# Experts 1 to 7 and the overflow tile in scaled f16 pairs, with the order of three engines in the experts laid down

## The chip, the cores and the metric

The kernel runs on one core of one Trainium2 chip. The metric is the device time of one execution in microseconds (us). TensorE multiplies (PE in the profile), ScalarE is ACT, VectorE is DVE, GpSimd is POOL, and SyncE (SP) issues most transfers.

## What is computed

Three blocks run one after the other: attention with a decay for 4 x 8 heads of 576 tokens, a swiglu layer for 2304 tokens, and a mixture of 8 experts in which each token goes to one expert. In the reference, cut to the last block:

```python
# x: 2304 x 512, w1: 8 x 512 x 1024, w2: 8 x 1024 x 512, all float32
logits = x @ w_gate
expert_idx = np.argmax(logits, axis=1)
probs = softmax(logits)
for e in range(8):
    mask = expert_idx == e
    h = np.maximum(x[mask] @ w1[e], 0.0)
    out[mask] = gate_w[mask, None] * (h @ w2[e])
```

`gate_w` is the probability of the chosen expert. The swiglu's output is `x` here, and everything is float32 in and out.

## The kernel before

**Up to 703 us** the kernel does the attention and the swiglu in 9 groups of 256 tokens; the order of its instructions is set by a list scheduler with its own estimates of times. As each group's swiglu is done, `fin0` copies its rows (ys, L711 and L712) and stores them as f32 in y_d; `fin1` and `fin2` turn them (yt), multiply by the gate's weights, take the best expert and give each token a place in a list of slots. From 703 to 727 us the last group is routed while TensorE works on the first 128 tokens of expert 0 (`filler`, L1152 to L1183).

**The experts** run in a loop over s = 0 to 8. An expert has 320 places, as tiles of 128, 128 and 64 rows; what does not fit goes to the overflow tile, s = 8. All products are made from pairs: a float32 value is split into a high part rounded to fp32r and a rest, and three products (high by high, high by low, low by high) are added. `mm1` makes the hidden layer h: for each of 8 blocks fk of 128 hidden values, 12 matmuls of 320 columns (L1347; 192 for expert 0), then ScalarE writes relu (L1352) and VectorE the rest in two pieces (L1354). `mm2` multiplies h by w2 for the three row tiles in 24, 24 and 16 matmuls of 512 columns (L1390); ScalarE scales the result by the gate into o (L1392, L1394), GpSimd scatters it to the output (L1136). There is one h buffer; three banks of PSUM turn for mm1, three for mm2.

**The weights** come as f32 in four pieces of 512 KB per matrix (two matrices an expert) into four buffers (wr, issued by SP); ScalarE copies the high part (L1101), VectorE subtracts the rest (L1102). **The tokens** of the next expert are gathered from y_d by GpSimd (L1204), their 16-bit words separated by GpSimd and VectorE (L1468), turned by DMA (L1471), put together by ScalarE and VectorE (L1475, L1476) and split (L93). For experts 0 and 1 TensorE turns them (L1215). For the overflow tile `gate_of` (L1483) works out the gate again.

The scheduler orders the loop too: it mixes the L1347 of one expert with the L1390 of the one before, and places the relus, copies and splits where its estimates put them.

## Time and profile before

| | us |
|---|---|
| median of 3 executions | 986.05 (984.83 to 986.61) |
| the profiled execution | 986.64 |
| its span in the trace | 984.8 |
| TensorE busy in the span | 901.6 (92%) |
| VectorE busy | 624.5 (63%) |
| ScalarE busy | 551.1 (56%) |
| attention and swiglu, up to the last group's routing | 703 |
| last routing, beside the filler | 703 to 727 |
| expert 0 and the entry to expert 1 | 727 to 757 |
| the rest of the experts and the overflow tile | 757 to 974 |
| last copy, scatter and end | 974 to 985 |

Times in rows are microseconds from the span's start. Matmuls are pipelined: the duration printed for one is longer than the distance to the next one, so a stream is priced by its length in the chain of waits over its count. An engine that is busy for almost all of a stretch sets its length; the others matter there only where something waits for them.

### The profile page before, as it was taken

What the parts mean: (1) busy time and instruction counts of PE and PEld (TensorE: products, weight loads), DVE (VectorE), ACT (ScalarE), POOL (GpSimd) and SP (SyncE); (2) the same over time, 40 slices, a digit from 0 to 9 for tenths busy, and PEclk for the clock granted to TensorE, in tenths of its full rate; (3) what the DMA queues carried; (4) which work ended last, traced back from release to release, by engine and by line L of the source; (5) the groups of instructions that cost most, each with busy time, mean ns of one, the idle gap of its engine ahead of it and who ended that gap; (6) DMA issues with size and microseconds to landing.
All of it is one profiled execution on the core that took longest, in us unless ns stands there. A gap on an engine that the chain in (4) does not pass through costs nothing.

```text
span 984.8 us, 20192 instructions
## 1 busy us (share of the span) xinstructions
PE 901.6 (92%) x7317; PEld 751.1 (76%) x7317; DVE 624.5 (63%) x1876; ACT 551.1 (56%) x1210; POOL 302.6 (31%) x366
## 2 busy tenths in 40 slices
PE   3688669879999999999999999999999999999995
PEld 2466447667788888888878788888888878988884
DVE  7998999888657555666643535445547676556540
ACT  6999997667566656666633322223425554555440
POOL 0110125336434434344442232232256432110011
PEclk9999777989999999999999999999999999999998
DMA  8615868889787687577655502102369875665410
GB/s 238 186 39 153 208 165 180 158 167 190 144 159 142 113 165 150 104 142 127 102 106 135 150 23 56 32 8 80 99 169 246 231 219 159 184 209 193 141 57 35
DMA packets 265496, 136.92 MB, mean 139 GB/s; under 512 B 228943, under 2 KB 241359, under 8 KB 265394
## 3 DMA queue, kind: packets, MB, share of 16 engines
q1 hardware_dynamic: 261136, 125.23, 54.6%
q0 software_dynamic: 4064, 10.24, 3.5%
q8 instruction: 58, 0.95, 0.4%
q14 instruction: 44, 0.36, 0.1%
q10 hardware_dynamic: 194, 0.14, 0.1%
HBM read 84.76 MB, written 10.82 MB: 97 GB/s over the span
## 4 chain that ended last, share of the span: by engine, by line
PE 42%; DMA 9%; issue 7%; DVE 3%; ACT 1%; POOL 1%; SPq 0%; POOLq 0%; DVEq 0%; ACTq 0%
PE yp L663 10%; PE v L601 9%; PE g L601 9%; PE bank L1347 4%; PE bank L1390 3%; DMA pair<-words 3%; DMA out_dram<-o,ix 3%; PE ps L322 1%; DMA pt<-p 1%; PE px L485 1%; DMA xg<-y_d,ix 1%; DVE wlo L1102 1%; DMA xr<-xs 1%; DVE wolo L1102 1%; PE ps L327 1%
## 5 line engine op out<-in xcount | busy, mean ns | idle before, releaser
L422 POOL TENSOR_TENSOR p<-st,p 128x128 f16<-128x128 f32 (+1 forms) x96 | 82.0, 857 | 115.2 <-issue 65.2
L648 POOL TENSOR_TENSOR lo<-t,hi 128x512 fp32r<-128x512 f32 x54 | 70.8, 1312 | 134.3 <-ACT hi L647 102.7
L601 PE MATMUL g<-xr,wga 128*128 128x256 f16 x864 | 104.6, 278 | 1.1 <-DVE t L634 1.1
L601 PE MATMUL v<-xr,wva 128*128 128x256 f16 x864 | 103.1, 273 | 0.6 <-DVE p L454 0.6
L389 ACT ACTIVATE st<-st,nb,c 128x64 f32<-128x64 f32 (+4 forms) x160 | 102.8, 645 | 1.4
L379 DVE CUSTOM_DVE_ANT_0 st<-ps,zero 128x64 f32<-128x64 f32 (+3 forms) x160 | 55.8, 376 | 70.5 <-PE ps L332 64.8
L601 PEld LDWEIGHTS <-wga 128*128 128x128 f16 x864 | 83.7, 100 | 17.6 <-issue 6.4
L601 PEld LDWEIGHTS <-wva 128*128 128x128 f16 x864 | 83.8, 100 | 10.2 <-issue 0.6
L631 ACT ACTIVATE t<-g,gscale 128x512 f32<-128x512 f32 (+3 forms) x72 | 39.4, 572 | 79.6 <-PE g L601 77.8
L419 DVE CAST p<-st 128x448 f16<-128x448 f32 (+3 forms) x120 | 48.7, 412 | 34.6 <-ACT st L389 32.8
L433 POOL TENSOR_TENSOR p<-st,p 128x64 f16<-128x64 f32 x96 | 43.0, 448 | 79.4 <-issue 34.9
L1136 POOL DMA_INDIRECT out_dram<-o,ix x24 | 24.8, 1033 | 126.5 <-ACT o L1392 81.6
L647 ACT ACTIVATE hi<-t 128x512 fp32r<-128x512 f32 x54 | 33.7, 624 | 52.0 <-DVE t L641 51.9
L322 PE MATMUL ps<-qkt 128*128 128x64 f16 (+4 forms) x288 | 53.7, 288 | 7.8 <-DVE mx L379 4.7
L663 PE MATMUL yp<-wohi,hi 128*128 128x512 f32 x144 | 59.5, 413 | 0.0
L1352 ACT ACTIVATE h<-bank 128x320 fp32r<-128x320 f32 (+1 forms) x64 | 26.1, 422 | 57.8 <-PE bank L1347 57.5
L1354 DVE SCALAR_TENSOR_TENSOR h<-bank,h 128x64 fp32r<-128x64 f32 (+2 forms) x128 | 33.4, 305 | 39.1 <-ACT h L1352 39.0
L663 PE MATMUL yp<-wohi,lo 128*128 128x512 f32 x144 | 56.9, 395 | 0.0
L663 PE MATMUL yp<-wolo,hi 128*128 128x512 f32 x144 | 56.3, 391 | 0.0
L327 PE MATMUL ps<-cum,nc 128*128 128x64 bf16 (+2 forms) x192 | 55.2, 294 | 0.0
L385 ACT ACTIVATE nb<-mx,addc,c 128x3 f32<-128x3 f32 (+1 forms) x64 | 24.7, 386 | 52.4 <-DVE mx L379 51.9
L641 DVE SCALAR_TENSOR_TENSOR t<-t,hscale,v 128x512 f32<-128x512 f32 (+3 forms) x72 | 42.4, 609 | 16.1 <-PE v L601 15.7
(372 smaller groups left out, 2554.5 us busy)
## 6 DMA issues: line engine op xcount, KB each, us to landing
wr<-in_moe_w_dram SPq DMA_DIRECT2D x72, 512.0 KB, 5.0
vr<-in_v_dram SPq DMA_DIRECT2D x16, 288.0 KB, 3.9
qk_in<-in_q_dram SPq DMA_DIRECT2D x32, 128.0 KB, 2.9
qk_in<-in_k_dram SPq DMA_DIRECT2D x32, 128.0 KB, 2.8
v_in<-in_v_dram SPq DMA_DIRECT2D x32, 128.0 KB, 2.7
y_d<-ys SPq DMA_DIRECT2D x6, 512.0 KB, 4.1
wgb<-in_moe_w_gate_dram SPq DMA_DIRECT2D x5, 512.0 KB, 5.2
raw<-in_moe_w_val_dram SPq DMA_DIRECT2D x5, 512.0 KB, 5.1
```

Of the source, the lines that this page charges most:

```text
L322: pe.matmul(out=ps[:, o:o + n], lhsT=lq[:, 128 * j:128 * j + 128], rhs=rk_[:, k0:k1], start=(x == 0), stop=False, skip_group_check=True,)
L327: pe.matmul(out=ps[:, o:o + n], lhsT=pk, rhs=cum3[:, k0 - 64:k1 - 64], start=False, stop=(k1 <= d0), skip_group_check=True,)
L379: vec.tensor_tensor_reduce(out=sts[m][:, k0 - 64:k1 - 64], in0=ps[:, o:o + n], in1=zero.to_broadcast([128, n]), scale=1.0, scalar=init, op ...
L389: act.activation(out=sts[m], in_=sts[m], func=ACTF.Exp, scale=c[:, 0:1], bias=nb[:, m:m + 1], accum_out=sm[:, m, hh:hh + 1],)
L419: vec.tensor_copy(out=flat[:, o + 64:o + 64 + n], in_=src)
L422: gp.tensor_tensor(out=flat[:, o1:o1 + n - 64], in0=src[:, 64:n], in1=flat[:, o + 128:o + 64 + n], op=ALU.subtract)
L433: gp.tensor_tensor(out=blk[:, :, 0:64], in0=pair, in1=blk[:, :, 64:128], op=ALU.subtract)
L601: pe.matmul(out=ps[:, fi, :], lhsT=w16[:, kk, wi, 128 * fi:128 * fi + 128], rhs=xr[:, kk, x0:x0 + 2, xi, :], start=(n_ == 0), stop=(n_ == ...
L631: act.activation(out=t[:, :, c0:c1], in_=gps[:, :, c0:c1], func=ACTF.Tanh, scale=gscale[:, b, j:j + 1])
L641: vec.scalar_tensor_tensor(out=t[:, :, c0:c1], in0=t[:, :, c0:c1], scalar=hscale[:, b, j:j + 1], in1=vps[:, :, c0:c1], op0=ALU.mult, op1=A ...
L648: last["lo"] = gp.tensor_tensor(out=lo, in0=t, in1=hi.bitcast(F32), op=ALU.subtract)
L663: pe.matmul(out=yps[g][i], lhsT=hx[:, fi, 128 * i:128 * i + 128], rhs=wo[fk][wx], start=(j in opens and n_ == 0), stop=(j in shuts and n_ ...
```

## The change

**Number format.** For experts 1 to 7 and the overflow tile the pairs become f16. To stay in the range of f16 each matrix is multiplied by a power of two. `load16` holds the steps: `square` sums the squares of a quarter of the matrix (ScalarE L1148, or VectorE L1143), `reduce` adds the four sums (VectorE L1155), `total` adds over partitions with a matmul of one column (TensorE L1159), `scale` takes the exponent with three small VectorE operations, and `convert` writes the high half (ScalarE L1170, a copy with a scale) and the low half (VectorE L1171). Expert 0 stays in fp32r.

**Tokens.** `fin1` sums the squares of each token's row (ScalarE, two operations a group), and `halves` writes both f16 halves of the row (two operations on ScalarE L748, two on VectorE L749) and stores them to a new array y16_d, 2304 x 1024 f16, 4.7 MB in all. Experts 1 and on gather from y16_d, and one DMA transpose per tile puts both halves in place: the separation of words, xf, the split and the TensorE transposes for expert 1 are gone. `gates` multiplies the gate by the inverse scales. The overflow's gate takes 4 matmuls and 4 transposes in place of 16 matmuls.

**Order.** In the expert stage `laid` ties every instruction of TensorE, ScalarE and VectorE to the one before it in the program's order. `plan` says after which block of mm1 (list a) and after which eight matmuls of mm2 (list b) squares, totals and conversions stand. SP and GpSimd are not tied.

**Buffers.** Raw weights stay in three places of one matrix each: the four wr buffers and two that held expert 0's w1 (free after expert 0's mm1). There are two token buffers, three o buffers and four f16 matrix pairs.

The diff, cut to its core:

```diff
+    y16_d = dram.tile([NT + 1, 2 * DM], F16, name="y16_d")
...
+    def halves(g, ys, yt, sc):
+        yh = yt.rearrange("p i k t -> p (i k t)").bitcast(F16).rearrange("p (i c) -> p i c", i=2)
+        for i in range(2):
+            hi = yh[:, i, 0:DM]
+            act.activation(out=hi, in_=ys[:, i, :], func=ACTF.Copy, scale=sc[:, i:i + 1])
+            vec.scalar_tensor_tensor(
+                out=yh[:, i, DM:], in0=ys[:, i, :], scalar=sc[:, i:i + 1], in1=hi, op0=ALU.mult, op1=ALU.subtract
+            )
+        rows_out(y16_d, g, yh)
...
+        sq = M["rt"].tile([128, 2, 2], F32, tag="ysq", name="ysq")
+        for i in range(2):
+            jk = M["rt"].tile([128, G], F32, tag="lgp", name="jk", bufs=1).bitcast(F16)
+            act.activation(out=jk, in_=ys[:, i, :], func=ACTF.Square, accum_out=sq[:, 0, i:i + 1])
+        exponent(sq[:, 1, :], sq[:, 0, :], sq[:, 0, :], 20, 11)
+        ytp[g] = (yt, lg, ys, sq)
...
+        if g < NG - 1:
+            halves(g, ys, yt, sq[:, 1, :])
...
+        if g == NG - 1:
+            halves(g, ys, yt, sq[:, 1, :])
...
+        act.dma_start(out=y16_d[NT:NT + 1, :], in_=zr.bitcast(F16))
...
+    def load16(s, which, src, psum, e_i=None):
+        n, cols = src.shape[-2] // 128, src.shape[-1]
+        step, k16 = 1024 // cols, len(turns16)
+        turns16.append((s, which))
+        q4 = EP["wq"].tile([128, 4], F32, tag="q4", name="q4")
+        sc = EP["wq"].tile([128, 1], F32, tag="wsc", name="wsc")
+        inv = inv16[s, which] = EP["winv"][:, k16 % 4:k16 % 4 + 1]
+        raw, stage = [], stages[(k16 - 2) % 3] if k16 > 1 and (k16 - 2) % 3 < 2 else None
...
+        def square(i, on_vec=False):
+            t = raw[i][1].rearrange("p k c -> p (k c)")
+            acc = q4[:, i:i + 1]
+            if on_vec:
+                jk = jd[0]
+                vec.tensor_tensor_reduce(
+                    out=jk, in0=t, in1=t, scale=1.0, scalar=0.0, op0=ALU.mult, op1=ALU.add, accum_out=acc
+                )
+            else:
+                jk = EP["wq"].tile([128, 1024], F16, tag="ja", bufs=1, name="ja")
+                act.activation(out=jk, in_=t, func=ACTF.Square, accum_out=acc)
+
+        tot = []
+
+        def reduce():
+            tot.append(EP["wq"].tile([128, 1], BF16, tag="qs", bufs=2, name="qs"))
+            with nc.allow_low_precision(reason="only picks a power of two"):
+                vec.tensor_reduce(out=tot[0], in_=q4, axis=AX.X, op=ALU.add)
+
+        def total():
+            tot.append(psum()[:, 0:1])
+            pe.matmul(out=tot[1], lhsT=ones, rhs=tot[0], start=True, stop=True, skip_group_check=True)
+
+        def scale():
+            exponent(sc, inv, tot[1], 20, 7 if which == 1 else 1)
+
+        def convert(i):
+            c, t = raw[i]
+            wt[s, which] = [
+                bufs16[k16 % 4][:, x].rearrange("p (k c) -> p k c", k=n) for x in range(2)
+            ]
+            h_, l_ = [x[:, c:c + step, :] for x in wt[s, which]]
+            act.activation(out=h_, in_=t, func=ACTF.Copy, scale=sc)
+            vec.scalar_tensor_tensor(out=l_, in0=t, scalar=sc, in1=h_, op0=ALU.mult, op1=ALU.subtract)
...
-                    EP["w1"] = [go() for go in load_w(1, 1, w1[1])]
+                    EP["w1"] = load16(1, 1, w1[1], lambda: ps_s.tile([128, 512], F32, tag="s", name="tot"))
+                    for i in range(4):
+                        EP["w1"]["sq"](i)
+                    for x in ("red", "mm", "exp"):
+                        EP["w1"][x]()
             elif g1 == NG - 1 and j1 == NJ - 1:
-                wbuf.append([wpa.tile([128, 4096], F32R, tag=x, name=x) for x in ("wga", "wva")])
+                bufs16.extend(wpa.tile([128, 2, 4096], F16, tag=x, name=x) for x in ("wga", "wva"))
                 with tc.issue_after(last["hi"].ins):
-                    for f_ in EP["w1"]:
-                        f_()
-                EP["w12"] = [go() for go in load_w(1, 2, w2[1])]
+                    for i in range(4):
+                        EP["w1"]["cv"](i)
...
+            if beat and n_ % 8 == 7 and n_ < len(prods) - 1:
+                beat()
...
-    def turn(xt, xs):
-        pair = tw_p.tile([128, 2 * KD, CAP], U16, tag="pair", name="pair")
+        return gather(xg_p, idx, None, y16_d if s else y_d)
+
+    def turn(s, xs):
         o = 0
-        for t, (x, n, _) in enumerate(xs):
-            words = tw_p.tile([128, 2, DM], U16, tag="words", name="words", bufs=2)
-            for w in range(2):
-                (gp, vec)[w].tensor_copy(
-                    out=words[0:n, w, :], in_=x[0:n, :].bitcast(U16).rearrange("p (d w) -> p d w", w=2)[:, :, w]
-                )
-            sp.dma_start_transpose(out=pair[:, :, o:o + n], in_=words[0:n].rearrange("p w d -> p (w d)"))
+        for x, n, _ in xs:
+            sp.dma_start_transpose(out=x16[s % 2][:, :, o:o + n], in_=x[0:n, :])
             o += n
-        xf = hs_p.tile([128, KD, CAP], F32, tag="hs", name="xf")
-        xw = xf.bitcast(U16).rearrange("p k (t w) -> p k t w", w=2)
-        act.activation(out=xw[:, :, 0:o, 0], in_=pair[:, 0:KD, 0:o], func=ACTF.Copy)
-        vec.tensor_copy(out=xw[:, :, 0:o, 1], in_=pair[:, KD:, 0:o])
-        split(xt[0][:, :, 0:o], xt[1][:, :, 0:o], xf[:, :, 0:o], xt[0][:, :, 0:o].bitcast(F32))
...
+    def plan(s):
+        m1, m2, m3 = 2 * s, 2 * s + 1, 2 * s + 2
+        a, b = [[[] for _ in range(9)] for _ in range(2)]
+        if s == 0:
+            a[1] = [("sq", 1, 0), ("sq", 1, 1, True)]
+            a[2] = [("sq", 1, 2), ("sq", 1, 3, True)]
+            a[4] = [("red", 1)]
+            a[6] = [("mm", 1)]
+            a[7] = [("exp", 1)]
+            b[0] = [("cv", 1, 0), ("cv", 1, 1)]
+            b[1] = [("cv", 1, 2), ("cv", 1, 3)]
+            b[3] = [("sq", 2, 0), ("sq", 2, 1, True)]
+            b[4] = [("sq", 2, 2), ("sq", 2, 3, True)]
+        else:
+            for i in range(4):
+                a[2 * i] = [("cv", m1, i)]
+                a[2 * i + 1] = [("sq", m2, i)]
+                b[3 + i] = [("cv", m2, i)]
+            if s == 1:
+                a = [
+                    [("red", 2), ("sq", 3, 0)], [("sq", 3, 1)], [("mm", 2), ("sq", 3, 2)], [("exp", 2), ("cv", 2, 0)],
+                    [("cv", 2, 1)], [("cv", 2, 2)], [("cv", 2, 3)], [("sq", 3, 3)],
+                ]
+            b[0] = [("sq", m3, 0), ("sq", m3, 1, True)]
+            b[1] = [("red", m2), ("sq", m3, 2), ("sq", m3, 3, True)]
+            b[2] = [("mm", m2)]
+            b[3].insert(0, ("exp", m2))
+            b[4] += [("red", m3)]
+            b[6] += [("mm", m3)]
+            b[7] += [("exp", m3)]
+        return a, b
...
+                    tc.add_manual_dep(
+                        ins, before[ins.engine].name,
+                        mybir.DependencyInfo(mybir.DependencyClass.NoSync, mybir.DependencyReason.DATA), reason="laid",
+                    )
+                before[ins.engine] = ins
...
+                mm1(fk, wt[s, 1], xt, bank, h, 0 if s else 128)
+                do(*pa.pop(0))
+                if fk == 3 and nxt is not None:
+                    turn(nxt, xgs[nxt])
+            if s:
+                ask(2 * s + 3)
...
+            stages.extend(EP["wq0"].tile([128, 4096], F32, tag=f"w{x}0", name="stage") for x in ("hi", "lo"))
+            ask(2)
+            ask(3)
...
```

ScalarE between one expert and the next, before (bank is PSUM; L1352 is the relu, L1394 the copy of the 64-row tile, L1101 and L1475 weights and tokens of later experts):

```order
L1352 ACTIVATE h<-bank_10515 128x320
L1394 ACTIVATE o<-bank_10503 64x512
L1352 ACTIVATE h<-bank_10495 128x320
L1352 ACTIVATE h<-bank_10511 128x320
...
L1101 ACTIVATE whi_9035<-wr 128x1024 x4
L1352 ACTIVATE h<-bank_10515 128x320
L93 ACTIVATE xh_10472<-xf 128x1280
L1475 ACTIVATE xf<-pair 128x1280
L1101 ACTIVATE wohi<-wr 128x1024 x2
L1392 ACTIVATE o<-bank_10507,ixf 128x512
```

and after (L1457 is the relu, L1170 a conversion, L1148 a square, L1505 and L1507 the copies to o):

```order
L1507 ACTIVATE o<-bank_10658 64x512
L1457 ACTIVATE h<-bank_10666 128x320
L1170 ACTIVATE wohi<-stage,wsc 128x1024
L1457 ACTIVATE h<-bank_10670 128x320
L1148 ACTIVATE ja,q_11372<-wr 128x1024
L1457 ACTIVATE h<-bank_10650 128x320
...
L1148 ACTIVATE ja,q_11518<-stage 128x1024 x2
L1505 ACTIVATE o<-bank_10662,sx_10636 128x512
L1170 ACTIVATE wolo<-wr,wsc 128x1024 x2
```

Relus stood in a row with the weights' copies in bunches; now one piece of weight work stands between any two relus, and each relu waits behind it.

TensorE where mm2 of one expert meets mm1 of the next, before:

```order
L1347 MATMUL bank_10515<-xh_10472,wva 128x320
L1390 MATMUL bank_10507<-whi_9035,h 128x512
L1390 MATMUL bank_10507<-wlo_9036,h 128x512
L1390 MATMUL bank_10499<-whi_9035,h 128x512
L1390 MATMUL bank_10499<-wlo_9036,h 128x512
...
L1347 MATMUL bank_10495<-xh_10472,wga 128x320
L1347 MATMUL bank_10495<-xl_10473,wga 128x320
```

and after (L1501 is mm2, L1159 the total, L1452 mm1; weight loads have rows of their own in f16):

```order
L1501 MATMUL bank_10658<-wva,h 128x512
L1159 LDWEIGHTS ones
L1159 MATMUL bank_10678<-qs,ones 128x1
L1501 LDWEIGHTS h
...
L1452 LDWEIGHTS wohi
L1452 MATMUL bank_10670<-x_0_10633,wohi 128x320
...
L1452 MATMUL bank_10650<-x_0_10633,wohi 128x320
```

Before, matmuls of two experts and of several row tiles were mixed; now mm1 runs block by block to its end, then mm2 tile by tile, with a total in between.

VectorE in the last group's routing, before (L712 and L754 are copies that the routing needs, L1102 weight work, L784 the first step of taking the best expert):

```order
L1102 TENSOR_TENSOR wva<-wr,wga 128x1024 x3
L712 COPY ys<-yp 128x512
L1102 TENSOR_TENSOR wva<-wr,wga 128x1024
L754 COPY yt<-ps 128x512
L784 TENSOR_REDUCE rmx<-ps 128x2
L786 SCALAR_TENSOR_TENSOR oh_10336<-ps,rmx,desc 128x8 x2
```

and after (the same steps are L713, L1171, L778, L815 and L817; L732 to L740 are the exponent, L749 the low halves):

```order
L1171 SCALAR_TENSOR_TENSOR wga<-wr,wsc,wga 128x1024
L713 COPY ys<-yp 128x512
L1171 SCALAR_TENSOR_TENSOR wga<-wr,wsc,wga 128x1024 x3
L778 COPY yt<-ps 128x512
L732 TENSOR_SCALAR ysq<-ysq 128x2
L737 TENSOR_SCALAR ysq<-ysq 128x2
L740 TENSOR_SCALAR ysq<-ysq 128x2
L749 SCALAR_TENSOR_TENSOR yt<-ys,ysq,yt 128x512
L815 TENSOR_REDUCE rmx<-ps 128x2
L749 SCALAR_TENSOR_TENSOR yt<-ys,ysq,yt 128x512
L817 SCALAR_TENSOR_TENSOR oh_10484<-ps,rmx,desc 128x8 x2
```

Three pieces of weight work instead of one stand between the copies ys and yt, and the halves stand on both sides of the step that takes the best expert.

## Rows read from the trace of the kernel before

**Rows 1.** Windows: stretch, length; busy (count) PE, PEld, DVE, ACT, POOL; clock, DMA share, GB/s.
```profile
0.00:160.00 160.00, 108.08 (x944) 78.05 (x945) 147.24 (x466) 143.16 (x368) 21.86 (x33) 0.87 0.63 165
220.00:545.00 325.00, 319.44 (x3137) 266.13 (x3136) 193.74 (x597) 192.27 (x479) 137.00 (x188) 1.00 0.71 138
545.00:703.00 158.00, 157.74 (x1268) 132.25 (x1268) 72.47 (x356) 42.54 (x77) 42.24 (x39) 1.00 0.22 58
703.00:727.00 24.00, 23.13 (x128) 17.63 (x125) 13.16 (x47) 10.58 (x17) 8.73 (x10) 1.00 0.51 139
727.00:757.00 30.00, 28.99 (x185) 26.56 (x186) 18.36 (x37) 15.09 (x24) 20.40 (x20) 0.94 0.81 204
757.00:974.00 217.00, 212.54 (x1156) 188.44 (x1156) 125.97 (x228) 104.32 (x147) 44.89 (x46) 1.00 0.57 170
```

**Rows 2.** Chain of waits, matmul streams at full clock: start, us, what, count.
```profile
347.77 2.64 PE g L601 x24
...
792.72 5.28 PE bank L1347 x36
...
890.23 11.71 PE bank L1390 x50
...
936.29 1.68 PE bank L1483 x16
```

**Rows 3.** TensorE timeline of an f16/bf16 stream: start, us, line, op, tiles, shapes, count.
```profile
221.08 0.60 PE L322 MATMUL ps<-qkt 128*128 128x512 f16 x2
221.52 0.38 PE L327 MATMUL ps<-cum,nc 128*128 128x512 bf16 x1
221.73 0.19 PE L332 MATMUL ps<-maskgt,negid 128*128 128x64 bf16 x1
```

**Rows 4.** TensorE's waits in 757 to 974: waiter, releaser: us in total, times, longest.
```profile
PE bank L1390 <- ACT h L1352: 2.7, 3, 1.5
PE bank L1390 <- DVE h L1354: 2.1, 4, 1.1
```

**Rows 5.** Groups by shape, 757 to 974: count | busy us, mean ns | idle before.
```profile
L1352 ACT ACTIVATE h<-bank 128x320 fp32r<-128x320 f32 x55 | 23.2, 436 | 47.5 <-PE bank L1347 47.2
...
L1101 ACT ACTIVATE wga<-wr 128x1024 fp32r<-128x1024 f32 x20 | 19.9, 1051 | 2.4 <-PE bank L1390 1.4 <-PE bank L1347 1.0
```

**Rows 6.** f16 weight work of the swiglu, by line: count, min/median/max ns.
```profile
L1016 ACT ACTIVATE wga<-c x4: 614/619/639, 19.1 to 108.3; 128x512 f16<-128x512 f32 x4
...
L1016 ACT ACTIVATION_READ_ACCUMULATOR wga<-c x4: 185/192/210, 19.6 to 108.8; 128x1 f32 x4
...
L1030 ACT ACTIVATE wga<-c,sw x4: 706/707/708, 35.9 to 126.2; 128x512 f16<-128x512 f32 x4
...
L1031 DVE SCALAR_TENSOR_TENSOR wga<-c,sw,wga x4: 733/738/743, 39.7 to 129.2; 128x512 f16<-128x512 f32 x4
```

**Rows 7.** VectorE timeline, last routing.
```profile
706.56 3.82 DVE L1102 TENSOR_TENSOR wva<-wr,wga 128x1024 fp32r<-128x1024 f32 x3 [1.65 <-ACT wga L1101]
...
710.31 0.68 DVE L712 COPY ys<-yp 128x512 f32<-128x512 f32 x1
...
712.04 0.68 DVE L754 COPY yt<-ps 128x512 f32<-128x512 f32 x1
```

**Rows 8.** ScalarE timeline, last routing.
```profile
709.28 0.57 ACT L711 ACTIVATE ys<-yp 128x512 f32<-128x512 f32 x1
```

**Rows 9.** TensorE timeline, entry to the experts.
```profile
727.08 0.58 PE L1347 MATMUL bank<-xh,whi 128*128 128x192 f32 x3 [0.47 <-ACT xh L93]
...
733.56 0.99 PE L1215 MATMUL bank<-ident,xg 128*128 128x128 f32 x8
```

**Rows 10.** DMA issues of the page: KB each, median us to landing.
```profile
wr<-in_moe_w_dram SPq DMA_DIRECT2D x72, 512.0 KB, 5.0
```

**Rows 11.** ScalarE timeline, first 20 us.
```profile
9.59 0.63 ACTq L919 DMA_DIRECT2D y_d<-zr  x1
...
14.14 0.66 ACT L998 ACTIVATE c<-raw 128x512 f32<-128x512 f32 x1 [1.03 <-DMA raw<-in_moe_w_gate_dram]
```

More of the change, by code (lines that the diff above doesn't have):

```diff
@@ L845, in fin2 @@
         if final:
-            place(0, 1)
+            place(0, NT3)
         step(g)
         if final:
-            vec.tensor_tensor(out=EP["ix"], in0=ixf[:, 0, :], in1=rk[:, 32:32 + NT3], op=ALU.add)
+            vec.tensor_tensor(out=EP["ix"], in0=ixf[:, 0:NT3], in1=rk[:, 32:32 + NT3], op=ALU.add)
         vec.tensor_tensor(out=cnt, in0=cnt, in1=rk[:, 2 * NE:3 * NE], op=ALU.add)
@@ L1340, with f32 @@
     LO = CAP + 64
+    def f32(x):
+        return x.bitcast(F32) if x.dtype == F32R else x
     def mm1(fk, w, x, ps, h, c0):
@@ L1375, in mm1s, with mm2 @@
             hi = hh[:, f0:f0 + 4, 0:128]
-            split(hi, hl[:, f0:f0 + 4, 0:128], p, hi.bitcast(F32))
-    def mm2(t, n, idx, gwt, w, hh, hl, ps, o_p):
+            split(hi, hl[:, f0:f0 + 4, 0:128], p, f32(hi))
+    def mm2(t, n, idx, gwt, w, hh, hl, ps, o_p, beat=None):
         p = ps("m2")
@@ L1417, in table @@
             )
-            tc.keep_in_program_order(first)
             oe = ov.tile([1, NE], F32, name="oe")
@@ L1452, in weights @@
         src = w1 if which == 1 else w2
-        return load_w(s, which, src[s]) if s < NE else load_w(s, which, src, reg["e"])
+        if s < NE:
+            return load16(s, which, src[s], lambda: banks[7])
+        return load16(s, which, src, lambda: banks[7], reg["e"])
     def fetch_x(s, t0=0):
@@ L1483, in gate_of @@
             pe.matmul(
-                out=p, lhsT=x[:, kk, 0:128].bitcast(F32), rhs=rg[:, kk, 0:NE], start=(n_ == 0),
+                out=p, lhsT=f32(x[:, kk, 0:128]), rhs=rg[:, kk, 0:NE], start=(n_ == 0),
                 stop=(n_ == len(prods) - 1), skip_group_check=True,
@@ L1495, in gate, with ask, do @@
     def gate(s, t):
-        return ixf[0:ROWS[t], 1, TPE * s + t:TPE * s + t + 1] if s < NE else gwo
+        n = ROWS[t] if s < NE else 128
+        return sx[s % 2][0:n, t:t + 1] if s else ixf[0:n, 2 * NE * TPE + t:2 * NE * TPE + t + 1]
+    asked = {}
+    def ask(m):
+        if m < 2 * NE:
+            asked[m] = weights(m // 2 + 1, m % 2 + 1)
+    def do(*items):
+        for what, m, *i in items:
+            if m in asked:
+                asked[m][what](*i)
+    def plan(s):
[11 more added lines that the diff above has]
+            b[4] = [("sq", 2, 2), ("sq", 2, 3, True)]
+        else:
+            for i in range(4):
[15 more added lines that the diff above has]
+        return a, b
@@ new lines, in laid @@
+    def laid():
+        body = nc.cur_bb.bb.instructions
+        before = {}
+        for ins in list(body)[n_before:]:
+            if ins.engine in LAID and not type(ins).__name__.startswith("BassTile"):
+                if ins.engine in before:
+                    tc.add_manual_dep(
+                        ins, before[ins.engine].name,
+                        mybir.DependencyInfo(mybir.DependencyClass.NoSync, mybir.DependencyReason.DATA), reason="laid",
+                    )
+                before[ins.engine] = ins
@@ L1510 @@
             sp.dma_start(out=ixo, in_=id_d[bass.ds(reg["r"], 128), :])
[L1511 to L1549 removed]
+    laid()
     p2.close()
```

204 lines of the change are left out of this document (131 added, 73 removed).

## The prediction, made before the change was run

> **What bounds the kernel now.** I read the windows first [rows 1]. From 220 us on TensorE is busy 97 to 100% of every stretch, at a granted clock of 1.00 except just after the entry to the experts (0.94). In the experts (757 to 974) it works 212.54 of 217 us; VectorE works 126, ScalarE 104, the DMA engines 57%. So the length of the expert stage is the number of matmuls times the distance between two of them, and the other engines count only where TensorE waits for them. Up to 160 us it is otherwise: ScalarE and VectorE work 143 and 147 of 160 us. Second, the waits: in those 217 us TensorE waits 4.8 us in all, for a relu or its rest [rows 4]. Third, the chain of waits gives lengths of unbroken streams, and so the distance [rows 2]: mm1 5.28/36 = 146.7 ns for 320 columns of fp32r, mm2 11.71/50 = 234.2 ns for 512 columns, and the swiglu's f16 2.64/24 = 110.0 ns for 256. The timeline has f16 and bf16 matmuls of 512 columns inside a stream, three in 0.65 us: 216.7 ns [rows 3].
>
> **Part 1, the number format on TensorE.** 320 columns in f16 lie between 256 and 512: 110.0 + 106.7 x 64/256 = 136.7 ns, 10.0 less than now. Seven experts x 96 x 10.0 ns = 6.7 us. In mm2, 7 x 64 x 17.5 ns = 7.8 us. The overflow tile has 48 matmuls of 512 columns: 0.8 us. The twelve transposes for expert 1, at 0.99/8 = 0.12 us [rows 9]: 1.5 us. The overflow's gate, at 1.68/16 = 0.105 us [rows 2]: twelve matmuls fewer, four transposes more, 0.8 us. Together 17.6 us.
>
> The Trainium skill bears on this, "TensorE: Matmul & The Clock Gate", section "Back-to-back issue gap": in a stream of weight load and matmul pairs, 512 columns come every 131 ns or so, and about 216 is for an isolated one. The rows here show 216.7 ns inside a stream that has its weight loads, so the trace disagrees. What it would give is a rival, below.
>
> **Part 2, the order on TensorE.** The 4.8 us of waits [rows 4] come where mm2 starts on an h that is not there. After, mm2's first tile runs through 8 blocks with three matmuls each, so the last block of h is wanted 21 x 0.217 = 4.6 us after mm1 ends; relu 0.44 [rows 5] plus the rest on VectorE and one piece of weight work of 1.1 to 1.4 us are done by then. I take all 4.8 us as gained; what hides it is this order, and without it they return. Added are 15 one-column totals. The nearest row is the 64-column matmul, 0.19 us long beside others [rows 3]; between 0 and 0.19 I take 0.07, as most of it overlaps: 1.0 us (0 to 2.9).
>
> **Part 3, ScalarE and VectorE in the experts.** They must keep under TensorE's new time per expert, 96 x 0.137 + 64 x 0.217 = 27.0 us. ScalarE has 104.3/7 = 14.9 now [rows 1]. Its eight copies of 1.05 us [rows 5] get a scale, which made 512 columns 0.707 in place of 0.619 [rows 6]: 1.14 each, or twice 0.707 = 1.41 at the dear end. Six squares are new: 1.05 + 0.19 to read the sum [rows 5, 6] = 1.24, or 2 x 0.619 + 0.19 = 1.43. So 14.9 + 0.7 + 7.4 = 23.0, at the dear end 14.9 + 2.9 + 8.6 = 26.4; the token copies that go are not even taken off. VectorE has 126/7 = 18.0; its lows go from 3.82/3 = 1.27 [rows 7] to at most 2 x 0.738 = 1.48 [rows 6], +1.7, two squares add some 2.6 and the small steps 1.2: 23.5. Both fit, so nothing is charged. Within mm1 it is tighter: a relu and one piece of work are 0.44 + 1.14 or 1.24, 1.58 to 1.68 us, against 12 x 0.137 = 1.64 on TensorE; three banks and the 4.6 us above take up what falls behind.
>
> **Part 4, weights and tokens.** A matrix has three places and is squared a half-expert after its load can start, so a load has about 13.5 us or more to land, against 5.0 for one of 512 KB [rows 10]. The exception is the entry. The two places in expert 0's w1 come free only when its mm1 ends, at about 738 (96 matmuls of 0.11 us after 727). Then 4 MB are asked for at once. At 204 GB/s [rows 1] a matrix takes 10.3 us, so the second one's pieces land from 751 at 2.6 us each; its first square stands behind expert 1's first relu, near 738 + 40 x 0.234 + 1.6 = 749, and the next ones 1.6 us apart. Relus stand behind those squares on ScalarE, TensorE behind the relus. The squares fall back by some 5 us in three blocks, and three banks (about 3 us) take up part. I charge 1.5 us, between 0 and 6. Before, TensorE's waits for h there were at most 1.5 us each [rows 4]. The words, xf and split work was off TensorE's path; its going brings nothing beyond the 4.8. SP's transposes for the next expert stand at the middle of mm1, 20 us ahead of need.
>
> **Part 5, the last routing.** Now the copy ys starts when three lows have ended (706.56 + 3.82) and yt follows after one more, at 712.04 [rows 7]. After, three lows stand between the two. The sums are ready at about 709.28, where ScalarE starts its half [rows 8]; so ys ends at 709.9, three lows end at 713.7 (1.27 each) to 714.3 (1.48), and yt is late by 1.7 to 2.3 us. I take 1.7. The second low half before the one-hot step adds up to 0.74 [rows 6]; I take 0.6. The filler doesn't get longer, so both show on TensorE before expert 0. Expert 0 now runs 0.58 us of high-half matmuls and then transposes while its low halves are made [rows 9]; after, the second matmul already wants the low half: 0.7 us (0 to 1.2). Together 3.0 us.
>
> **Part 6, up to 703 us.** A group's routing gets two squares and two high halves on ScalarE (about 3 us) and as much on VectorE, and 0.5 MB more to store. From 220 to 703 us they are busy 235 and 266 of 483 us beside a full TensorE, so this hides; where they are full, before 160, no group is routed. There only a further transfer (0.63 us of ScalarE's queue) and the order at the start, where a 0.66 us copy comes ahead of the first head's [rows 11], count: 1.0 us. The scheduler also gives a different order over the whole stretch. Its price has no row; TensorE's free time from 0 to 160, 52 us, shows that there is room both ways, and I bound it at -4 and +6.
>
> **The sum.** Gains 17.6 + 4.8 = 22.4. Costs 1.0 + 1.5 + 3.0 + 1.0 = 6.5. Net 15.9: the span goes from 984.8 to 968.9. The profiled execution took 986.64, 1.84 over its span, and stands 0.59 over the median: 968.9 + 1.84 - 0.59 = **970.1 us**.
>
> **The rivals.**
> - *A wait at each handover.* For: in the laid order TensorE stops at a total, at the last block of h and at a new expert's weights, whatever else could run; within mm1 ScalarE has no slack. Against: per expert there is slack of 4 us and 3.5 us. With 1.0 us at each of 14 matrices, between 0 and the 1.5 of [rows 4]: 970.1 + 14 = 984.1.
> - *Phase 1 is worse laid.* For: ScalarE and VectorE are full in its first 160 us. Against: from 220 on TensorE is full whatever the order. At +9 more: 979.
> - *Loads lag (the slower side).* If the 4 MB at the entry never let the loads get ahead, each of 14 matrices would be squared behind its last landing, with ScalarE's relus queued behind. It decides from 16/14 = 1.1 us per matrix on; at the 2.6 us of one landing, 970 + 36 = 1006, less what banks absorb, about 15: 991. Against: after the entry the expert needs 4.2 MB in 27 us, 155 GB/s, under the 204 that were moved [rows 1].
> - *f16 is no faster in pairs.* Then 15.3 us are missing: 985.4. Against: [rows 2, 3].
> - *Matmuls overlap further.* Were 512 columns to come every 131 ns, as that section of the Trainium skill has it, mm2 would lose another 7 x 64 x 85 ns = 38 us: 932. By rows, as a mechanism: it needs a weight load hidden better than in the streams of [rows 2, 3], and these show none.
>
> **How the numbers follow.** Forecast 0.74, wait at each handover 0.08, phase 1 0.08, loads lag 0.05, no faster 0.03, further overlap 0.02. The low end has the re-ordering at -4, totals, entry and low-half cover at nothing: 970.1 - 4 - 1.0 - 1.5 - 0.7 - 1.0 (start) - 2 (part of the routing) = 960. The high end takes re-ordering +6, the entry at 6 (+4.5) and dear lows (+1): 981.6, and with part of the first rival 983. The range is 960 to 983, which leaves out the last three cases and half of the first rival. A measurement of this kernel tells 0.2%, 2 us, from no change: faster means under 984.1. Faster: 0.74 + 0.08 + 0.02 and half of the first rival, with a little of the forecast's own tail taken off: 0.88; within 0.2%: the no-faster case and the other half, 0.06; slower: 0.06.
>
> **What would show it.** Right: mm2's streams at about 217 ns and mm1's at 137; TensorE's busy share over 98% from 760 on; an expert in 27.0 us where it took 29.1; the first mm1 matmul of expert 0 some 2 us later against the last yp matmul than now; ScalarE idle a little in each mm2. Wrong: waits of TensorE on a total or a bank at each expert (first rival); squares that begin when a transfer lands (third); a distance of 234 ns in mm2 (fourth); 545 us reached late (second). The forecast falls if f16's distance in these matmuls isn't the swiglu's, or if the laid order costs more than 1 us per matrix.

## The result, and the profile after

The changed kernel takes 974.73 us (median of 4 executions, 974.1 to 976.29) beside 986.12 before: ratio 0.9889, 95% interval 0.9872 to 0.9906. That is 11.4 us less; 16 were forecast, and the range held it. The profiled execution took 974.1 us with a span of 972.1 (before 986.64 and 984.8).

Set against the trace of before, the span's 12.7 us split up like this. The marks are the first filler matmul (the end of the swiglu), the first matmul of expert 0 and the last matmul of all; starts in us:

| stretch | before | after | change | forecast |
|---|---|---|---|---|
| start to first filler matmul | 709.06 | 714.08 | +5.0 | +1.0 |
| to the first matmul of expert 0 | 18.02 | 20.27 | +2.3 | +2.3 |
| to the last matmul | 246.02 | 224.89 | -21.1 | -19.2 |
| to the end of the span | 11.70 | 12.89 | +1.2 | 0 |

The expert stage gave more than forecast; the rest of the program gave 8.5 us of it back, where 3.3 were charged. These are the windows of the changed kernel that answer to [rows 1], with the same columns (stretch, length, busy and count of PE, PEld, DVE, ACT, POOL, clock, DMA share, GB/s):

```profile
545.00:703.00 158.00, 157.99 (x1241) 130.96 (x1240) 89.25 (x407) 65.06 (x127) 42.19 (x38) 1.00 0.29 84
703.00:727.00 24.00, 22.50 (x142) 17.34 (x140) 16.75 (x57) 14.47 (x24) 4.75 (x5) 1.00 0.58 164
727.00:757.00 30.00, 28.48 (x176) 25.25 (x175) 13.70 (x38) 12.73 (x23) 17.39 (x18) 0.94 0.88 202
757.00:957.00 200.00, 198.39 (x1189) 115.17 (x1188) 135.83 (x307) 143.89 (x224) 40.40 (x34) 1.00 0.66 192
```

ScalarE and VectorE do more work in the experts than before, and TensorE is still busy throughout: the added work is beside it. The chain of waits (start, us, what, count) answers to [rows 2] and shows one whole expert and the next one's mm1:

```profile
785.71 13.04 PE bank L1452 x96
798.75 5.18 PE bank L1501 x24
803.93 0.00 PE bank L1159
803.94 6.93 PE bank L1501 x32
810.87 0.00 PE bank L1159
810.87 1.75 PE bank L1501 x8
812.62 13.04 PE bank L1452 x96
```

mm1 is 13.04/96 = 135.8 ns a matmul, mm2 5.18/24 = 215.8 and 6.93/32 = 216.6 ns, and a total (L1159) shows as 0.00. By the starts of the matmuls it isn't quite free: from 790 us on the mm2 matmul behind a total starts 244 ns after the one ahead of it, where 216 ns is the rule (11 of 11). From 785.7 to 920 experts 2 to 6 take 26.9 us each without a gap; among expert 7's matmuls stand those of the overflow tile. Against [rows 4], all waits of TensorE from 757 on (waiter, releaser: us, times, longest):

```profile
PE bank L1452 <- DVE h L1459: 1.4, 2, 1.1
PE bank L1159 <- DVE qs L1155: 0.2, 1, 0.2
```

The weight work, by shape, from 785 on (count | busy us, mean ns | idle before), to be read beside [rows 5, 6]:

```profile
L1148 ACT ACTIVATE ja<-stage 128x1024 f16<-128x1024 f32 x24 | 25.2, 1051 | 0.3
...
L1171 DVE SCALAR_TENSOR_TENSOR wohi<-stage,wsc,wohi 128x1024 f16<-128x1024 f32 x8 | 10.3, 1285 | 4.4 <-ACT wohi L1170 4.4
...
L1170 ACT ACTIVATE wolo<-stage,wsc 128x1024 f16<-128x1024 f32 x9 | 10.0, 1137 | 0.8 <-DVE wsc L740 0.8
```

A square takes 1.05 us, a scaled conversion 1.14, a low half 1.28: the middle values of part 3, not the dear ends.

### The profile page after: what moved, and what is told of

The parts are those of the page before. It is cut to its first block, busy times and chain, and to the rows that moved or that the text cites. A ratio compares the mean times of both kernels' runs of the same rounds, so it can differ in the third digit from the quotient of the medians.

```text
span 972.1 us, 20385 instructions
## 1 busy us (share of the span) xinstructions
PE 889.3 (91%) x7317; PEld 674.4 (69%) x7317; DVE 649.8 (67%) x2019; ACT 613.4 (63%) x1346; POOL 288.4 (30%) x348
## 4 chain that ended last, share of the span: by engine, by line
PE 68%; DVE 10%; ACT 8%; DMA 7%; issue 4%; SPq 2%; POOL 1%; POOLq 0%; DVEq 0%; ACTq 0%
PE yp L664 13%; PE v L602 13%; PE g L602 11%; PE bank L1501 10%; PE bank L1452 10%; PE ps L323 3%; PE px L486 2%; DMA pt<-p 2%; ACT st L390 2%; DVE st L380 1%; DMA stage<-in_moe_w_dram 1%; PE px L477 1%; PE ps L328 1%; DVE p L455 1%; DVE qks L295 1%
## 5 line engine op out<-in xcount | busy, mean ns | idle before, releaser
L602 PE MATMUL v<-xr,wva 128*128 128x256 f16 x864 | 106.5, 279 | 2.7 <-DVE p L455 2.7
L1501 PEld LDWEIGHTS <-h 128*128 128x128 f16 x448 | 42.9, 98 | 50.1
L1233 POOL DMA_INDIRECT out_dram<-o,ix x24 | 27.0, 1126 | 112.8 <-ACT o L1505 56.8
L1501 PE MATMUL bank<-wva,h 128*128 128x512 f16 x256 | 56.4, 379 | 0.0
L1452 PE MATMUL bank<-x,wga 128*128 128x320 f16 x384 | 53.3, 299 | 1.4 <-DVE h L1459 1.4
```

The costliest lines, as they stand in the source:

```text
L602: pe.matmul(out=ps[:, fi, :], lhsT=w16[:, kk, wi, 128 * fi:128 * fi + 128], rhs=xr[:, kk, x0:x0 + 2, xi, :], start=(n_ == 0), stop=(n_ == ...
L1452: pe.matmul(out=p, lhsT=w[wi][:, kk, 128 * fk:128 * fk + 128], rhs=x[xi][:, kk, c0:CAP], start=(n_ == 0), stop=(n_ == 3 * KD - 1),)
L1501: pe.matmul(out=p[0:m, :], lhsT=hx, rhs=wx, start=(n_ == 0), stop=(n_ == len(prods) - 1))
```

## Where 8.5 us were given back

**The last routing.** TensorE's timeline (start, us, what, idle before):

```profile
714.08 0.39 PE L1249 MATMUL p<-whi,xh 128*128 128x512 f32 x1
...
716.84 1.09 PE L773 MATMUL ps<-ident,ys 128*128 128x128 f32 x8 [1.21 <-ACT ys L712]
...
734.35 0.36 PE L1452 MATMUL bank<-xh,whi 128*128 128x192 f32 x1 [0.47 <-ACT xh L94]
...
734.94 0.35 PE L1452 MATMUL bank<-xl,whi 128*128 128x192 f32 x1 [0.23 <-DVE xl L94]
```

VectorE's, to be read beside [rows 7]:

```profile
715.02 3.67 DVE L1171 SCALAR_TENSOR_TENSOR wga<-wr,wsc,wga 128x1024 f16<-128x1024 f32 x3
...
718.61 0.68 DVE L778 COPY yt<-ps 128x512 f32<-128x512 f32 x1
...
721.94 0.74 DVE L749 SCALAR_TENSOR_TENSOR yt<-ys,ysq,yt 128x512 f16<-128x512 f32 x1
...
727.93 0.18 DVE L879 TENSOR_TENSOR ix<-ixf,rk 128x24 int32<-128x24 f32 x1 [0.35 <-PE rk L869]
```

The copy yt (L778) starts 4.53 us after the first filler matmul, where it started 2.98 after (712.04 - 709.06): late by 1.55 us, behind three low halves, as priced (1.7). The second half of the halves (L749) stands before the one-hot step. The slot list (L879) comes 13.85 us after the first filler matmul, where it came 12.19 us after. The first filler matmul, the slot list and the gather in the kernel before:

```profile
709.06 0.40 PE L1152 MATMUL p<-whi,xh 128*128 128x512 f32 x1
...
721.25 0.18 DVE L849 TENSOR_TENSOR ix<-ixf,rk 128x24 int32<-128x24 f32 x1 [0.76 <-PE rk L838]
...
721.70 0.99 POOL L1204 DMA_INDIRECT xg<-y_d,ix  x1 [6.77 <-DVE cnt L850]
```

In the changed kernel GpSimd adds something that was not foreseen:

```profile
728.37 0.27 POOL L1522 IOTA thr<- 1x128 f32 x1 [8.81 <-DMA y_d<-yt]
728.60 0.30 POOL L1527 IOTA ii<- 1x128 f32 x1
729.10 0.99 POOL L1303 DMA_INDIRECT xg<-y_d,ix  x1 [0.20 <-issue]
```

Two index operations for the overflow table stand ahead of the gather of expert 0. They waited 8.81 us for the store of the halves (in the releaser's name, yt is the tile that holds the halves), presumably because they take over its memory, and the gather goes out 1.17 us after the slot list; before, it was 0.45 us.

**The entry.** ScalarE's timeline in expert 1:

```profile
761.79 1.06 ACT L1148 ACTIVATE ja<-stage 128x1024 f16<-128x1024 f32 x1 [2.12 <-DMA stage<-in_moe_w_dram]
762.76 0.19 ACT L1148 ACTIVATION_READ_ACCUMULATOR ja<-stage 128x1 f32 x1
762.85 0.41 ACT L1457 ACTIVATE h<-bank 128x320 f16<-128x320 f32 x1
763.17 1.04 ACT L1148 ACTIVATE ja<-stage 128x1024 f16<-128x1024 f32 x1
```

A square waits 2.12 us for its transfer and stands ahead of a relu, as part 4 described. Expert 1's mm1 takes 15.1 us, 2.1 more than the later ones; 1.5 were charged.

**The tail.** The last copy and scatter after, and then before:

```profile
959.66 0.69 ACT L1505 ACTIVATE o<-bank,sx 128x512 f32<-128x512 f32 x1 [3.61 <-PE bank L1501]
961.39 0.98 POOL L1233 DMA_INDIRECT out_dram<-o,ixo  x1 [2.35 <-DMA out_dram<-o,ix]
```

```profile
973.57 0.69 ACT L1392 ACTIVATE o<-bank,gwo 128x512 f32<-128x512 f32 x1 [4.89 <-PEq L1557]
974.54 0.97 POOL L1136 DMA_INDIRECT out_dram<-o,ixo  x1 [3.43 <-ACTq L1557]
```

The overflow's 24 matmuls now come right behind the 64-row tile of expert 7. The scatter of that tile is still under way when the last one is ready, so that the last goes out 1.73 us after its copy's start; before, it was 0.97. That is 0.8 of the 1.2 us; the rest lies behind the start of the last scatter (10.7 us to the end of the span, before 10.3), and nothing here explains it. No step of the prediction looked at the tail.

## Experiments

Each kernel was timed beside the kernel before on its own chip. The chips differ by some us, so times are compared on one chip only; what is smaller than the intervals is read from the traces.

| kernel | us, median | before, same chip | ratio (95% interval) |
|---|---|---|---|
| e1, laid order removed | 1007.72 | 988.73 | 1.016 (1.0111 to 1.0209) |
| e3, before with halves | 994.5 | 988.73 | 1.004 (1.0011 to 1.0069) |
| e10, before with zero row | 990.82 | 988.73 | 1.0014 (0.9985 to 1.0044) |
| e8, before with laid order | 1044.56 | 988.73 | 1.0558 (1.0506 to 1.0611) |
| e4, conversions late | 978.36 | 990.03 | 0.9861 (0.9822 to 0.9899) |
| e6, squares late | 974.51 | 990.03 | 0.9825 (0.9786 to 0.9864) |
| e9, gather first | 988.4 | 990.03 | 0.998 (0.9951 to 1.0009) |
| e7, these three | 984.12 | 990.03 | 0.9919 (0.9884 to 0.9953) |
| f1, changed kernel again | 974.6 | 986.13 | 0.9862 (0.9828 to 0.9897) |
| f2, index operations moved | 972.68 | 986.13 | 0.9855 (0.9826 to 0.9885) |
| e12, zero row late | 970.87 | 986.13 | 0.9831 (0.9799 to 0.9862) |
| f3, combined | 966.51 | 986.13 | 0.9806 (0.9773 to 0.9839) |

### Is it the format or the order?

**e1** leaves the expert stage to the scheduler:

```diff
-    laid()
     p2.close()
```

> The changed kernel without the laid order: the scheduler orders the expert stage, all else (f16 pairs, halves, plan's positions as program order) stays, and the order up to the last routing is the same. Theory (the laid order is worth the 4.8 us of waits that it was priced at, and lets squares and relus alternate): 3 to 8 us slower than the changed kernel, 978 to 983 us, with TensorE waits for h or for squares back in the expert stage. Rival (the format alone makes the gain and any order keeps TensorE full): within 2 us of 974.7.

It came out 19 us slower than the kernel before on that chip, where the changed kernel gained 11 on its own: some 30 us from one to the other, far past the 3 to 8 of the theory. In the traces 24.4 us more lie between the first and the last matmul of the experts, and 10.4 us more between the first filler matmul and expert 0 (30.67 us in place of 20.27): there too a square stands ahead of a copy that the routing needs, and ScalarE waits 3.13 us for its transfer. Its waits in the experts (740 to 1000):

```profile
ACT ja L1148 <- DMA stage<-in_moe_w_dram: 32.7, 14, 6.2
...
DVE jd L1143 <- DMA stage<-in_moe_w_dram: 19.7, 9, 7.0
...
PE bank L1501 <- ACT h L1457: 13.6, 6, 6.0
```

The scheduler put squares ahead of relus before their transfers had landed: ScalarE waited 32.7 us for transfers in front of squares, VectorE 19.7, the relus stood behind, and TensorE waited for h, up to 6.0 us at a time, after which its granted clock was at half level for 3.4 to 6.8 us (at 807, 841 and 902). So the order isn't worth the 4.8 us of [rows 4], but all that the new weight work would cost without it. The third rival's mechanism is real; it is the laid order that keeps it out after the entry.

**e8** lays the order without format and plan:

```diff
+    def laid():   # the same function, in the kernel before
...
+    laid()
     p2.close()
```

> The kernel before with the same laid order (each instruction of TensorE, ScalarE and VectorE in the experts behind the one before it in the program), without the f16 pairs and without a plan that places the weight work. Theory (the order by itself is worth little; it needs the weight work spread between relus): weight copies in bunches hold the relus up, TensorE waits 1 to 3 us at each of 7 experts, 990 to 1005 us. Rival (laying the order is the gain): 981 to 983 us.

It came out 56 us slower than the kernel before on that chip, well past the range. TensorE's waits:

```profile
PE bank L1483 <- ACT xh L93: 10.0, 1, 10.0
...
PE bank L1347 <- ACT xh L93: 9.8, 7, 3.0
...
PE bank L1347 <- DVE h L1354: 7.5, 4, 3.2
```

The program of before issues token splits and copies in bunches; in that order TensorE waits for the next expert's tokens (xh) and for h at each expert. The theory had that; it left out the 10.0 us before the overflow's gate and the clock. All waits together are 38.8 us (5.6 in the kernel before), and from 782 on TensorE is at half level for 40.9 us, which takes away another 20. Format without order costs 19 us, order without a plan 56, both together with the plan gain 11: as times the parts can't be priced apart and added. No run has the plan with the old format. What the format gives can only be read from the distances: 672 mm1 matmuls at 10.9 ns less and 448 mm2 matmuls at some 18 ns less make 15.4 us.

### What cost 5 us before the experts?

**e10** adds only a transfer of 2 KB to the kernel before. The scheduler then gives the first 20 us another order, which runs on to the first routing and is that of the changed kernel. **e3** adds the halves too.

```diff
         act.dma_start(out=y_d[NT:NT + 1, :], in_=zr)
+        act.dma_start(out=y16_d[NT:NT + 1, :], in_=zr.bitcast(F16))
```

> The kernel before plus one transfer of 2 KB on ScalarE's queue in the first 20 us (the zero row of y16_d); no halves, no other work. Its order up to the first routing is that of the changed kernel. Theory (order): the loss up to 703 us is here too, 3.5 to 5 us, time 989.5 to 991, with TensorE at half clock for 3.4 us near 244 and near 271 us. Rival (the halves' squares, copies and stores make the loss): 986 to 987, as before.

> The kernel before plus the token halves of the change (squares, halves, the store to y16_d and its zero row); nothing reads them, and the experts stay in fp32r. Theory (what was lost up to 703 us is the other order of the scheduler, not the halves' work): the last swiglu matmul of the last group ends about 5 us later than in the kernel before, as in the changed kernel, with half-clock stretches after 220 us; time 990 to 993. Rival (the halves' work delays it): the same time, but then the kernel with only the zero row (e10) shows no loss.

The times are 2.1 and 5.8 us over before, the first within its interval. The profile of e10 shows the first filler matmul at 707.75, no loss at all, that of e3 at 711.97, 2.9 us later than before and not 5. So e10's median lies in the range of its theory, but its trace doesn't show the loss that the theory spoke of (its profiled execution was the fastest of ten, 987.4 to 996.0). What e3 does show is the last routing: 20.55 us from the first filler matmul to expert 0, as in the changed kernel (20.27), with 18.05 in e10. Halves alone can make that term: in e3 the slot list comes 14.08 us after the first filler matmul (12.22 in e10).

**e12** turns it round: the changed kernel, with the early order of before.

```diff
-        act.dma_start(out=y16_d[NT:NT + 1, :], in_=zr.bitcast(F16))
...
             rows_out(y_d, g, ys, True)
+            sp.dma_start(out=y16_d[NT:NT + 1, :], in_=y_d[NT:NT + 1, :].bitcast(F16))
```

> The changed kernel with the zero row of y16_d written by SP with the first group's rows, and not by ScalarE's queue at the start; the order up to the first routing is then that of the kernel before. Theory (the order at the start makes the loss up to 450 us): the last swiglu matmul comes 3 to 4 us earlier than in the changed kernel, near 710, without half-clock stretches between 220 and 300 us; 970 to 972 where the changed kernel has 974.7. Rival (the halves' transfers and the new code make it): no change, 714.

**f1** is the changed kernel on the same chip:

> The changed kernel as it is, once more, beside the three below on one chip. Theory: the last swiglu matmul of the last group again near 714 us, with half-clock stretches of 3.4 us near 244 and 271, experts 2 to 7 at 26.9 us each; time as before (974 to 979, as the chip's own level goes).

f1 came as expected: 974.6 us, the two stretches near 244 and 271, experts 2 to 6 at 26.9 us each.

e12 is 3.7 us faster than f1, 970.87 beside 974.60 (968.7 to 972.4 and 970.6 to 975.7, so the traces have to decide), and its first filler matmul starts at 709.97 where f1 has 715.12. Not all of these 5.15 us arrive: the way from there to expert 0 takes 23.94 us in place of 20.36. The windows show where they come from. The changed kernel, 220 to 280 us:

```profile
220.00:250.00 30.00, 28.33 (x257) 22.62 (x258) 26.75 (x90) 26.32 (x67) 16.48 (x24) 0.94 0.92 179
250.00:280.00 30.00, 27.05 (x259) 21.27 (x258) 17.07 (x49) 16.58 (x43) 13.52 (x19) 0.94 0.74 142
```

and e12:

```profile
220.00:250.00 30.00, 27.32 (x281) 22.77 (x282) 24.58 (x75) 24.90 (x64) 16.47 (x21) 1.00 0.91 188
250.00:280.00 30.00, 29.89 (x302) 25.01 (x303) 19.34 (x60) 18.46 (x47) 13.39 (x18) 1.00 0.76 146
```

In the changed kernel TensorE's granted clock is 0.94 in both (one stretch of 3.4 us at half level in each, near 244 and 271), in e12 1.00. But windows from 220 on leave out what lies just ahead of them: before is at half level for 6.8 us from 213 on, e12 for 3.4 us near 204 and near 215, the changed kernel for 3.4 us near 162 and near 206. So here is the whole stretch, for before, the changed kernel, e12 and e10:

```profile
160.00:300.00 140.00, 129.28 (x1291) 106.30 (x1290) 107.46 (x312) 96.80 (x237) 65.39 (x83) 0.98 0.84 166
160.00:300.00 140.00, 128.44 (x1224) 103.71 (x1225) 108.95 (x305) 95.16 (x233) 61.08 (x81) 0.95 0.86 164
160.00:300.00 140.00, 129.31 (x1280) 106.42 (x1288) 108.04 (x312) 96.47 (x235) 65.99 (x84) 0.98 0.85 168
160.00:300.00 140.00, 127.95 (x1279) 104.73 (x1278) 108.96 (x306) 95.47 (x232) 63.09 (x83) 0.98 0.86 166
```

The changed kernel is at half level for 13.6 us in it, the other three for 6.8. All 14 traces fall into two groups. Five have a clock of 0.98 here: the four with the early order of before (before, e8, e12, f3), and e10. Their 301st output matmul starts between 445.35 and 447.27 us (447.27 in before). The other nine, all with the changed kernel's early order, have 0.94 to 0.96, and theirs starts between 449.53 and 452.93 (451.02 in the changed kernel). A stretch at half clock takes away half its length, so the 6.8 us more make 3.4 of the 3.8 us that the changed kernel is behind at this mark.

Three things follow. The work of the halves can't have made this loss: its first instruction, a square (L784), runs at 505 us. The order at the start is the cause of it: e12 changes nothing else, and the loss is gone. But the order doesn't always lose: up to 300 us the rows of TensorE, ScalarE and VectorE come in the same order in e10's trace as in the changed kernel's, and yet TensorE was at half level no longer than before. Why that execution escaped is open.

The other 1.3 us come after the mark and stay open in part. There the gate's product (72 fp32 matmuls, L764 before and L793 after) takes 6.8 us in place of 5.1, by its starts; e3, which has the halves, has 5.1 too.

### The last routing and the entry

**e4** puts the conversions of expert 1's w1 behind the last routing's copies:

```diff
-                with tc.issue_after(last["hi"].ins):
-                    for i in range(4):
-                        EP["w1"]["cv"](i)
...
             halves(g, ys, yt, sq[:, 1, :])
+            with tc.issue_after(last["hv"].ins), tc.issue_after(last["ix"].ins):
+                for i in range(4):
+                    EP["w1"]["cv"](i)
...
```

> The changed kernel with the four conversions of expert 1's w1 moved behind the last routing's copies (ScalarE: behind the filler's splits; VectorE: behind the slot list), and expert 0's part of the plan shifted to fit. Theory (the conversions between ys and yt hold the routing): the slot list comes 1.5 to 3 us earlier against the last swiglu matmul, 972 to 973.5. Rival (GpSimd's queue has two small operations ahead of the gather that wait for the store of the halves): the slot list comes earlier but the gather doesn't follow in full, 973.5 to 975.

The slot list came 12.4 us after the first filler matmul, 1.4 earlier, as the theory has it; with the conversions away, the halves cost it 0.2 us (1.9 in e3, where the old weight copies stand beside them). Yet the first matmul of expert 0 came 2.0 us later, counted from the same mark:

```profile
PE bank L1317 <- DMA xg<-y_d,ix: 4.0, 2, 2.0
```

Expert 0 has two gathers. The first went out 0.45 us after the list, the second at 729.71, and the second landed 6.0 us after it went out (3.0 in the changed kernel). TensorE waited 2.0 us for each, and its clock was at half level for 10.2 us from 734 on. What made the gathers slow isn't settled; the loads of w2, released later by the same edit, are a candidate that no run isolates.

**e6** moves squares of expert 2's w2 behind the conversions:

```diff
-                    [("red", 2), ("sq", 3, 0)], [("sq", 3, 1)], [("mm", 2), ("sq", 3, 2)], [("exp", 2), ("cv", 2, 0)],
-                    [("cv", 2, 1)], [("cv", 2, 2)], [("cv", 2, 3)], [("sq", 3, 3)],
+                    [("red", 2)], [], [("mm", 2)], [("exp", 2), ("cv", 2, 0)], [("cv", 2, 1)], [("cv", 2, 2)],
+                    [("cv", 2, 3)], [("sq", 3, 0), ("sq", 3, 1, True)],
...
```

> The changed kernel with the squares of expert 2's w2 moved from expert 1's first blocks to its last block and its mm2, behind the conversions of expert 2's w1. Theory (ScalarE's relus stood behind squares whose transfers had not landed): TensorE's two waits of 1.4 us in all and the slow blocks near 763 to 770 go, expert 1's mm1 takes 13.0 to 13.3 us in place of 15.1, 972.5 to 973. Rival (the wait moves to the total at mm2's 24th matmul, since the transfers are late all the same): 974 to 975.

Expert 1 takes 27.8 us in place of 29.1 (28.3 in f1), and its mm1 13.1 in place of 15.1, as the theory has it: its waits go. A shorter one comes at the total, as the rival has it:

```profile
PE bank L1159 <- DVE qs L1155: 0.7, 1, 0.7
```

In that execution expert 0 took 1.4 us longer than in the changed kernel's trace, in a part that the edit doesn't touch (23.5 us, in f1 23.4), so the time alone doesn't show the gain: 974.51.

**e9** keeps the index operations behind the gathers; only GpSimd's order changes.

```diff
-            gp.iota(
+            tc.keep_in_program_order(gp.iota(
                 thr, [[0, NE], [128, MAXOV]], base=CAP + 1, channel_multiplier=0,
...
```

> The changed kernel with GpSimd's two index operations of the overflow table kept behind the gathers of experts 0 and 1. Theory: the gather of expert 0 follows the slot list after 0.3 to 0.5 us in place of 1.2, all of it on the path: 973.7 to 974.1. Rival (the gather waits for something else that ends as late): no change.

The gather did follow the slot list after 0.45 us, but at 988.4 us this was the slowest form of the changed kernel that keeps the laid order. TensorE's wait, and VectorE's row behind it:

```profile
PE bank L1159 <- DVE qs L1155: 5.3, 1, 5.3
```

```profile
809.99 0.28 DVE L1531 TENSOR_TENSOR gge<-cnt,thr 1x128 f32<-1x128 f32 x1 [5.52 <-POOL thr L1522]
```

The operations now stood behind all of GpSimd's transfers up to expert 2; VectorE's laid order waited 5.52 us for them in expert 2, a total's sum stood behind that, and TensorE behind the total, with its clock at half level for 6.8 us after. An engine outside the laid order can hold those that are in it.

**e7** joins the three and has this wait too:

> All three edits together in the changed kernel (conversions late, squares late, gather first). Theory (three separate waits): the gains add up, 969 to 971. Rival (they hide one another): no better than the best single one, 972 to 973.

Neither came: 984.12 us. TensorE waits 5.1 us at the same total in expert 2, and 3.5 us for the gathers, as in e4.

**f2** puts the operations between the gathers of experts 1 and 2:

```diff
             xgs[nxt] = fetch_x(nxt)
+        if s == 0:
+            tc.keep_in_program_order(gp.iota(EP["thr"], ...))
+            tc.keep_in_program_order(gp.iota(EP["ii"], ...))
```

> The changed kernel with GpSimd's two index operations of the overflow table between the gathers of expert 1 and expert 2 (in the earlier try they stood behind nearly all gathers, and VectorE, whose order is laid down, waited 5.5 us for them in expert 2). Only GpSimd's order differs. Theory: the gather of expert 0 follows the slot list after 0.3 to 0.5 us in place of 1.2, and nothing waits for them later: 0.5 to 0.8 us faster than the changed kernel on this chip. Rival (the wait only moves, as in the earlier try): same or slower by up to 8 us.

GpSimd's timeline (the gather of expert 0, and the first index operation):

```profile
727.61 0.98 POOL L1303 DMA_INDIRECT xg<-y_d,ix  x1 [8.75 <-DVE cnt L880]
...
733.60 0.27 POOL L1684 IOTA thr<- 1x128 f32 x1
```

The slot list started at 727.16, the gather 0.45 us after it. Expert 0 comes 19.6 us after the first filler matmul, 20.4 in f1: 0.7 us, as the theory has it, and nothing waits for the operations later. The medians differ by 1.9 us, less than the executions of f1 scatter; in the traces f2 is also 1.8 us ahead at the first filler matmul, where the two programs are the same.

**f3** combines e12, f2 and e6:

> The changed kernel with the zero row late, the index operations behind the gathers of expert 1, and the squares of expert 2's w2 late. Theory (three separate places): the gains add, 3.5 + 0.7 + 1.3, 5 us faster than the changed kernel on this chip, 969 to 970 at the level of the first runs. Rival (the entry's loads or the clock take it back): 1 to 2 us faster.

966.51 us, 8.1 under the changed kernel on the same chip and 19.6 under the kernel before: the fastest of all. The gather goes out at 723.63, 0.45 us after the slot list. In e12, by contrast, the slot list was there at 723.82 and the gather left only at 728.28, behind the index operations. With all three, TensorE's clock doesn't fall at the entry (f1 is at half level there for 6.8 us), and expert 0 takes 20.5 us in place of 23.4. That gain had no price, and so more than the sum of the three came: against f1's trace, 5.8 us up to the first filler matmul, 0.7 to expert 0, 2.9 in expert 0 and 0.6 in expert 1. Why the clock stays up isn't shown: f2 waits as briefly for its gather (0.3 us), and has 3.4 us at half level.

## Why the prediction was right or wrong

- **Part 1** was right: 135.8 and 216 ns where 136.7 and 216.7 were taken. The Trainium skill's figure of 131 ns for 512 columns in a stream ("TensorE: Matmul & The Clock Gate", "Back-to-back issue gap") isn't seen in 448 matmuls that each have their weight load; the 216 ns that the section calls isolated is what the stream has.
- **Part 2** was right for this kernel: the waits for h are gone from 770 on. The totals, charged 0.07 us each and 1.0 in all, cost 0.03 each, some 0.4.
- **Part 3** was right: TensorE doesn't wait for ScalarE or VectorE from expert 2 on, and the operations took the middle prices.
- **Part 4** had the place and the mechanism; 2.1 us where 1.5 were taken (f1: 1.4).
- **Part 5** came to 2.25 us where 2.3 and 0.7 were charged, but not of the same pieces: yt was late by 1.55, the slot list by 1.66 in all, 0.7 was GpSimd's queue, and the second matmul of expert 0 started 0.59 us after the first. GpSimd's queue was not looked at there.
- **Part 6** is the term that was mis-sized: 1.0 taken, 5.0 measured. "I bound it at -4 and +6" held the value, and so the range held the time. That the scheduler gives another order was seen, but with no row for its price it was put at nothing. The runs showed a loss of 3.8 us at 451 us, 3.4 of it by 6.8 us more at half level between 160 and 300 us, and 1.3 us after that, open in part. The order by itself could not have told this: e10 has the order and not the loss.
- **The tail** was left out: 1.2 us.
- **The rivals.** A wait at each handover and lagging loads did not come in this kernel; e9 and e1 show both in kernels next to it. Phase 1 worse laid is the one that came in part.
- The sum: 974.7 where 970.1 was forecast. Of the 4.6 us, 3.2 are in the span (972.1 for 968.9): +4.0 in part 6 and +1.2 in the tail, less the 1.9 that the experts gave beyond the forecast (0.9 of these are distances a little shorter than taken, 0.6 the totals; the rest isn't split). It was luck that these two misses partly cancel. The other 1.4 are that this profiled execution lies 0.6 us under its median, where that of before lay 0.6 over its own.

## What to carry to other kernels

Price a change that lays down an order together with the work that it places: either alone can cost more than both gain. An engine left out of the order (here GpSimd with two operations of 0.3 us) can still hold the engines in it, so look for what stands in its queue before the transfer that the path needs. Where a scheduler orders a long stretch ahead of the edit, a transfer of 2 KB can reshuffle it; if the stage that was meant gains as forecast and the total doesn't, compare the times at marks ahead of the stage first.
